# High parts of queries and keys loaded by casting transfers, a third fold in the feature transform, and a new order of the work

## The chip, the cores and the metric

The kernel runs on one core of a Trainium2 chip. The metric is the device time of one execution in microseconds (us); the median of three runs before the change is 947.48 us (945.76 to 948.42). A smaller time is better.

## What is computed

The reference is attention with capped scores, then a two-dimensional Fourier transform added to its input, a normalisation, and a two-layer feed-forward step with a residual. Four batches, 12 heads, 448 tokens, 64 values a head; 768 features, 3072 hidden features.

```python
scores = cap * tanh((q @ k.T) / sqrt(64) / cap)
attn = exp(scores - max(scores)); attn = attn / (sum(attn) + 1e-9)
x = (attn @ v), heads side by side           # 4 x 448 x 768
u = x + real(fft(fft(x, axis=1), axis=2))    # tokens, then features
un = (u - mean(u)) / sqrt(var(u) + 1e-6)     # over the features
out = u + max(un @ w_ch1, 0) @ w_ch2
```

## The kernel before

**Engines.** TensorE (PE in the profile) multiplies, VectorE (DVE) and ScalarE (ACT) do the elementwise work, GpSimd (POOL) does a few small steps, SyncE (SP) issues nearly all transfers. Each engine takes its instructions strictly in the order in which they stand.

**Attention.** The work goes by pairs of heads, 24 of them (`p`). `load_qk` brings queries and keys of a pair (128 x 964 floats) into `qkr`, three buffers deep, `load_v` brings the values. A product in full precision is put together from rounded parts: `split_q` and `split_k` round queries and keys to a high part, `qhl[:, 0]` on VectorE (L312) and `khl[:, 0]` on ScalarE (L310); `rest_q` and `rest_k` subtract it from the full value and so make the low part on VectorE (L315). There are two buffers of `qhl` and of `khl`, used by turns, so the parts of pair p are written into the buffers of pair p - 2, once that pair's scores have been read from them. A pair's 448 keys make seven units of 128 keys for one head or 64 for both; `scores` (L402) computes two units at a time (84 steps `t`), six matmuls each: low keys by high queries, high by low, high by high, summed in PSUM. `tanh` (L412) and `exp` (L415) are one ScalarE instruction each per step. `weigh` (L434) multiplies a unit with the values and a column of ones, `denominators` (L449, L450) and `normalise` (L456) divide.

**Transform, once a batch (six pairs).** The Fourier transforms are matmuls with constant matrices, made smaller by folding the input on its symmetries. `fold_tokens` (L475) and `mirror` (L481) fold tokens and features once; `fold_features` (L489) folds the features a second time, into sums (for even outputs) and differences (for odd outputs). `stage1` (L504) transforms the tokens, `combine` (L310, L524) puts even and odd parts together, `stage2` (L532) transforms the features: for each of its 16 calls, eight matmuls of two passes each, half of them with 192 odd output columns and half with 194 even ones. `add_u` (L552, L556) adds the result; `moments`, `rows`, `standardise` (L565, L574 to L583 on POOL, L610) normalise; `u_cols` (L619) transposes into `xc`, and `operand` and `operand_rest` split that as the queries were split.

**Feed-forward.** 12 groups of hidden features, four batches each: `up` (L745, L756, L757) and `down` (L774, L783). The weights come as raw double words (`raw`, transfer at L651) that the chip turns into a high and a low part: steps `first`, `second` and `third` of each of 96 pieces (L664 to L696, with a cast at L310 on ScalarE).

**Order.** Each step above (`split_q` of a pair, `scores` of two units, one weight step) is a call with a number in the table `ORDER`; the calls are sorted by that number, and so each engine's instructions are put in that order. `at` checks that what a call needs stands ahead of it. The feed-forward work of groups 1 to 11 does not stand in the table; its order follows from a rule that the change leaves alone.

## Time and profile before

| | before |
|---|---|
| median of 3 runs | 947.48 us |
| lowest, highest | 945.76, 948.42 us |
| profiled execution, its time | 947.62 us |
| its span (first to last instruction) | 945.5 us |
| granted TensorE clock, mean | 0.999 |
| TensorE busy | 920.4 us, 97% |
| VectorE busy | 732.4 us, 77% |
| ScalarE busy | 361.5 us, 38% |
| transfers | 64.65 MB |

Busy shares are means over stages that differ: ScalarE's 38% is an engine nearly always busy in the first 210 us and seldom after. A busy time counts an instruction from its start to its end; matmuls overlap, so TensorE can be called busy while the next matmul in line waits a little. How fast a stretch of matmuls goes is better read from many of them without a gap. A releaser (after `<-`) is the instruction or transfer whose end came last before a waiting instruction started.

### The profile page before, as it was taken

The page shows a single profiled execution, that of the slowest core. Times are in us where ns is not written, and L with a number is a line of the kernel's source. Part 1 is how long each engine was busy: PE and PEld are TensorE (multiplying, and loading weights), DVE is VectorE, ACT ScalarE, POOL GpSimd, SP SyncE. Part 2 cuts the span into 40 slices and gives each one's busy share as a digit, 9 for nine tenths or more (in the row PEclk, how much of TensorE's full clock was granted, in tenths as well). Part 3 has the DMA queues.
Part 4 walks back from the last instruction along what each step waited for, and adds up shares of the span by engine and source line. Part 5 has one row for each costly group of instructions (what it writes and reads, how often), then busy time and mean ns, then how long its engine had stood idle before and what let it go on. Part 6 is the DMA issues. An engine that isn't in the chain of part 4 may idle for free.

```text
span 945.5 us, 18375 instructions
## 1 busy us (share of the span) xinstructions
PE 920.4 (97%) x7648; PEld 821.2 (87%) x7648; DVE 732.4 (77%) x1486; ACT 361.5 (38%) x563; POOL 17.0 (2%) x47
## 2 busy tenths in 40 slices
PE   6999999998999999999999999999999999999998
PEld 4777778787888999999999999999999999999997
DVE  3589887899888877787887878778777777768633
ACT  7999999994612212221122211222112221122100
POOL 0000101010100000000000000000000000000000
PEclk9999999999999999999999999999999999999999
DMA  5454332310101211121111211112111211121033
GB/s 152 129 153 135 106 91 54 119 32 20 60 27 51 67 60 51 51 78 51 60 51 51 77 51 51 50 55 64 51 51 51 64 55 51 51 57 60 17 113 122
DMA packets 44914, 64.65 MB, mean 68 GB/s; under 512 B 24608, under 2 KB 29472, under 8 KB 44832
## 3 DMA queue, kind: packets, MB, share of 16 engines
q1 hardware_dynamic: 44752, 63.24, 22.0%
q8 instruction: 60, 0.98, 0.4%
q10 hardware_dynamic: 80, 0.25, 0.1%
q14 instruction: 22, 0.18, 0.1%
HBM read 57.96 MB, written 5.52 MB: 67 GB/s over the span
## 4 chain that ended last, share of the span: by engine, by line
PE 83%; ACT 7%; DVE 7%; issue 2%; DMA 0%; POOL 0%; SPq 0%; DVEq 0%; ACTq 0%; POOLq 0%
PE ph L745 37%; PE po L774 37%; PE av L434 4%; PE s L402 3%; ACT a L412 3%; ACT a L415 2%; PE pq L532 2%; DVE y L524 1%; ACT u L610 1%; DVE bs L565 1%; DVE u L456 1%; DMA capt<-cap 0%; ACT xc L310 0%; ACT khl L310 0%; DVE tf L475 0%
## 5 line engine op out<-in xcount | busy, mean ns | idle before, releaser
L774 PE MATMUL po<-hh,w 128*128 128x448 f32 x1728 | 361.7, 367 | 1.9 <-DVE xc L783 1.4
L745 PE MATMUL ph<-xs,w 128*128 128x448 f32 x1728 | 358.6, 366 | 0.0
L774 PEld LDWEIGHTS po<-hh,w 128*128 128x128 f32 x1728 | 322.9, 188 | 34.2 <-DVE xc L783 5.1
L745 PEld LDWEIGHTS ph<-xs,w 128*128 128x128 f32 x1728 | 323.9, 188 | 27.2 <-issue 0.6
L783 DVE TENSOR_TENSOR xc<-xc,po 128x448 f32<-128x448 f32 x288 | 176.4, 617 | 44.5 <-PE po L774 44.1
L664 ACT ACTIVATE wt<-raw 128x384 f32<-128x384 f32 x96 | 53.4, 557 | 243.5 <-DVE w L696 243.5
L757 DVE SCALAR_TENSOR_TENSOR hh<-ph,hh 128x448 fp32r<-128x448 f32 x96 | 59.9, 624 | 96.2 <-ACT hh L756 95.8
L756 ACT ACTIVATE hh<-ph 128x448 fp32r<-128x448 f32 x96 | 52.3, 545 | 170.0 <-PE ph L745 170.0
L434 PEld LDWEIGHTS av<-vt,a 128*50 128x50 f32 (+3 forms) x3072 | 84.4, 130 | 18.3 <-issue 11.0
L310 ACT CAST w<-wt 128x384 fp32r<-128x384 f32 x96 | 49.2, 513 | 130.2 <-DVE wt L671 130.2
L434 PE MATMUL av<-vt,a 128*50 128x65 f32 (+3 forms) x3072 | 92.0, 223 | 4.0 <-issue 1.7
L402 PE MATMUL s<-qhl,khl 64*128 64x452 f32 (+1 forms) x504 | 78.5, 399 | 11.2 <-DVE khl L315 8.5
L415 ACT ACTIVATE a<-a,capt 128x904 f32<-128x904 f32 x84 | 85.7, 1056 | 0.6
L412 ACT ACTIVATE a<-s,tscale 128x904 f32<-128x904 f32 x84 | 83.4, 1018 | 4.3 <-PE s L402 3.2
L402 PEld LDWEIGHTS s<-qhl,khl 64*128 64x128 f32 (+1 forms) x504 | 50.1, 190 | 26.3 <-DVE khl L315 8.8
L671 DVE SCALAR_TENSOR_TENSOR wt<-wt 128x384 f32<-128x384 f32 x96 | 53.6, 558 | 10.7 <-DVE wt L668 0.9
L668 DVE SCALAR_TENSOR_TENSOR wt<-raw,wt 128x384 uint32<-128x384 uint32 x96 | 53.6, 559 | 3.3
L690 DVE SCALAR_TENSOR_TENSOR wt<-raw,wt 128x384 f32<-128x384 uint32 x96 | 53.6, 558 | 3.3
L696 DVE TENSOR_TENSOR w<-wt 128x384 fp32r<-128x384 f32 x96 | 53.5, 558 | 3.3
L315 DVE TENSOR_TENSOR wt<-wt,w 128x384 f32<-128x384 f32 x96 | 52.8, 550 | 0.7 <-ACT w L310 0.7
L665 DVE TENSOR_SCALAR wt<-raw 128x384 uint32<-128x384 uint32 x96 | 34.1, 355 | 1.2
L687 DVE TENSOR_SCALAR wt<-wt 128x384 uint32<-128x384 uint32 x96 | 33.9, 353 | 0.5
(58 smaller groups left out, 380.6 us busy)
## 6 DMA issues: line engine op xcount, KB each, us to landing
raw<-w2r SPq DMA_DIRECT2D x48, 384.0 KB
raw<-w1r SPq DMA_DIRECT2D x48, 384.0 KB
qkr<-qkT SPq DMA_DIRECT2D x23, 482.0 KB
vt<-vr SPq DMA_DIRECT2D x24, 224.0 KB
outT<-xc SPq DMA_DIRECT2D x24, 224.0 KB
dev<-lnrow SPq DMA_DIRECT2D x4, 224.0 KB
mean<-lnrow SPq DMA_DIRECT2D x4, 224.0 KB
featT<-feat SPq DMA_DIRECT2D x2, 386.0 KB
```

The lines of the kernel that those rows point to most:

```text
L402: nc.tensor.matmul(ps_t[t][:, i, :SQ], khl[p % 2][rows, ik, k0 : k0 + P], qhl[p % 2][rows, iq], start=(k_ == 0), stop=(k_ == 2),)
L412: nc.scalar.activation(a_t[t], ps_t.pop(t)[:, :, :SQ], AF.Tanh, scale=tscale)
L415: nc.scalar.activation(a_t[t], a_t[t], AF.Exp, scale=capt)
L434: nc.tensor.matmul(pa_t[p][q0:q1, j, g * (D + 1) : (g + 1) * (D + 1)], a_t[t][rows, n, OFF[g] + q0 : OFF[g] + q1], vt[rows, p % 2, i], sta ...
L668: nc.vector.scalar_tensor_tensor(tu, hi.bitcast(U32), 0xC0000000, tu, op0=ALU.bitwise_and, op1=ALU.bitwise_or)
L671: nc.vector.scalar_tensor_tensor(t, w, HI_MIN, t, op0=ALU.is_ge, op1=mul)
L690: nc.vector.scalar_tensor_tensor(w, lo, 2.0**-52, w, op0=mul, op1=mul)
L696: nc.vector.tensor_tensor(ws[c][1][:, sl], t, w, op=add)
L745: nc.tensor.matmul(ph[:, :S], w_[:, dc * P : (dc + 1) * P], x_, start=(k_ == 0), stop=(k_ == 3 * NDC - 1),)
L757: nc.vector.scalar_tensor_tensor(hh[:, 1], ph[:, :S], 0.0, f32(hh[:, 0]), op0=ALU.max, op1=sub)
L774: nc.tensor.matmul(po[:, :S], w_[:, dc * P : (dc + 1) * P], hh[:, x_], start=(k_ == 0), stop=(k_ == 3 * GF - 1),)
L783: nc.vector.tensor_tensor(ac, ac, po[:, :S], op=add)
```

## The change

- The high parts of queries and keys are no longer made by ScalarE and VectorE from `qkr`. POOL issues a transfer for each that reads queries or keys from DRAM and casts them on the way into `qhl` and `khl` (48 transfers). The rests still read `qkr`. A cast needs the scores of the pair two before, as before, and no longer the load of `qkr`.
- Within a step of scores the order of the three products is turned: high by high, high keys by low queries, low keys by high queries.
- The even half of the features is folded a third time. `fold_features` does the odd half first; for the even half it folds in place and then makes two sets of 97 columns, by outputs 0, 4, 8, ... and 2, 6, 10, ... `stage1` takes the two sets in its two halves. `stage2` computes 97 even columns from each set, where it summed 194 columns over two halves; they are written to every second column of PSUM, so `add_u` is as before. The constant matrix is filled to match.
- All numbers of `ORDER` are new.

```diff
 ORDER = {
...
     "split_k": [
-        6, 13, 45, 54, 78, 113, 153, 168, 231, 258, 290, 308, 358, 392, 438, 481, 502, 527, 564, 588, 663, 696,
-        742, 761
+        10, 20, 31, 63, 80, 126, 167, 174, 230, 261, 273, 320, 350, 378, 420, 483, 500, 553, 565, 631, 665, 690,
+        751, 768
     ],
...
 ENGINES = {
-    "k": "AAAA",
-    "q": "DDDD",
     "standardise": "AAAA",
...
-            feat[n, :FW, p, NJO : NJO + len(j_even)] = half * f(2 * np.pi * ((d * j_even) % DM) / DM)
             feat[n, :FW, p, :NJO] = half * f(2 * np.pi * ((d * j_odd) % DM) / DM)
+            d, j = np.arange(FW)[:, None], j_even[p::2]
+            feat[n, :FW, p, NJO : NJO + len(j)] = np.where(d == FW - 1, 0.5, 1.0) * f(2 * np.pi * ((d * j) % DM) / DM)
...
     def split_q(p):
-        copy("q", p // NP, qhl[p % 2][:, 0], qk[p][:, :SQ])
+        nc.gpsimd.dma_start(qhl[p % 2][:, 0], qkT[p // NP, PAIRS[p % NP], :, :SQ])
...
     def split_k(p):
-        copy("k", p // NP, khl[p % 2][:, 0], qk[p][:, SQ:])
+        nc.gpsimd.dma_start(khl[p % 2][:, 0], qkT[p // NP, PAIRS[p % NP], :, SQ:])
...
-        terms = (1, 0), (0, 1), (0, 0)
+        terms = (0, 0), (0, 1), (1, 0)
...
-            f_t[b, sd] = new([P, 4, NF], F32, "ff", 2, "ff")
-        t = t_t[b][:R, n]
-        nc.vector.tensor_tensor(
-            f_t[b, sd][:R, 2 * n : 2 * n + 2],
-            t[:, :, :NF],
-            t[:, :, DM // 2 : DM // 4 - 1 : -1],
-            op=(add, sub)[sd != n],
-        )
+            f_t[b, sd] = new([P, 4, 2 * FW], F32, "ff", 2, "ff")
+        t, f, m = t_t[b][:R, n], f_t[b, sd][:R, 2 * n : 2 * n + 2], DM // 4
+        if sd:
+            nc.vector.tensor_tensor(f[:, :, :NF], t[:, :, :NF], t[:, :, 2 * m : m - 1 : -1], op=(add, sub)[n == 0])
+            return
+        nc.vector.tensor_tensor(t[:, :, :m], t[:, :, :m], t[:, :, 2 * m : m : -1], op=(add, sub)[n])
+        for p in range(2):
+            nc.vector.tensor_tensor(
+                f[:, :, p * FW : (p + 1) * FW], t[:, :, :FW], t[:, :, m : FW - 2 : -1], op=(add, sub)[p != n]
+            )
...
-        for sd, (j0, nj) in enumerate(SDJ):
-            for p in range(2):
-                for q0, q1 in ((0, D), (D, R)):
-                    nc.tensor.matmul(
-                        ps[q0:q1, j0 : j0 + nj],
-                        y_t[b, p][:FW, sd, k0 + q0 : k0 + q1],
-                        featT[n][:FW, p, j0 : j0 + nj],
-                        start=(p == 0),
-                        stop=(p == 1),
-                    )
+        for sd, p in (1, 0), (1, 1), (0, 0), (0, 1):
+            out = ps[:, :NJO] if sd else ps[:, NJO + p : NJO + 2 * FW : 2]
+            for q0, q1 in ((0, D), (D, R)):
+                nc.tensor.matmul(
+                    out[q0:q1],
+                    y_t[b, p][:FW, sd, k0 + q0 : k0 + q1],
+                    featT[n][:FW, p, :NJO] if sd else featT[n][:FW, p, NJO : NJO + FW],
+                    start=(sd == 0 or p == 0),
+                    stop=(sd == 0 or p == 1),
+                )
...
-            at(f, p, needs=[("load_qk", p)] + ([(first.__name__, p)] if first else [("scores", u // 2) for u in units(p - 2)]))
+            at(f, p, needs=[("load_qk", p), (first.__name__, p)] if first else [("scores", u // 2) for u in units(p - 2)])
```

What the new order makes of an engine's instructions is shown at three places. A row is source line, operation, output and inputs, shape of the output, and how many follow each other.

ScalarE from its first cast on, before (`khl` are keys, `wt` and `w` a weight piece, `s` scores, `a` the tile of tanh and exp):

```order
L310 CAST khl<-qkr 128x512
L664 ACTIVATE wt<-raw 128x384
L310 CAST khl<-qkr 128x512
L412 ACTIVATE a<-s,tscale 128x904 x2
L415 ACTIVATE a<-a,capt 128x904
L412 ACTIVATE a<-s,tscale 128x904 x2
L415 ACTIVATE a<-a,capt 128x904 x3
```

and with the change (its line numbers are lower by 2 here):

```order
L664 ACTIVATE wt<-raw 128x384
L308 CAST w_113<-wt 128x384
L410 ACTIVATE a<-s,tscale 128x904
L413 ACTIVATE a<-a,capt 128x904
L410 ACTIVATE a<-s,tscale 128x904 x2
L413 ACTIVATE a<-a,capt 128x904
```

The key casts are gone, here and wherever else they stood, and the first weight piece's cast, which stood behind the twelfth tanh, now stands ahead of the first.

VectorE at its first steps for the scores, before (the three `wt` rows are step `first` of a weight piece):

```order
L312 CAST qhl<-qkr 128x452
L315 TENSOR_TENSOR khl<-qkr,khl 128x512
L315 TENSOR_TENSOR qhl<-qkr,qhl 128x452
L665 TENSOR_SCALAR wt<-raw 128x384
L668 SCALAR_TENSOR_TENSOR wt<-raw,wt 128x384
L671 SCALAR_TENSOR_TENSOR wt<-wt 128x384
```

and with the change:

```order
L665 TENSOR_SCALAR wt<-raw 128x384
L668 SCALAR_TENSOR_TENSOR wt<-raw,wt 128x384
L671 SCALAR_TENSOR_TENSOR wt<-wt 128x384
L313 TENSOR_TENSOR qhl<-qkr,qhl 128x452
L313 TENSOR_TENSOR khl<-qkr,khl 128x512
```

The weight steps moved ahead of the two rests.

VectorE in the last batch's transform, from the last token folds (`tf`) on, before (`ff` are the twice folded features, `xs` an operand of the feed-forward step, `y` the transformed tokens):

```order
L475 TENSOR_TENSOR tf<-u 114x4x128 x2
L481 TENSOR_TENSOR tf<-tf 114x2x383
L489 TENSOR_TENSOR ff<-tf 114x386
L481 TENSOR_TENSOR tf<-tf 114x2x383
L489 TENSOR_TENSOR ff<-tf 114x386
L315 TENSOR_TENSOR xs<-xc,xs 128x448
L489 TENSOR_TENSOR ff<-tf 114x386 x2
L524 TENSOR_TENSOR y<-yps,yh 97x2x113 x8
```

and with the change:

```order
L473 TENSOR_TENSOR tf<-u 114x4x128 x2
L479 TENSOR_TENSOR tf<-tf 114x2x383 x2
L488 TENSOR_TENSOR ff<-tf 114x2x193 x2
L490 TENSOR_TENSOR tf<-tf 114x2x192
L492 TENSOR_TENSOR ff<-tf 114x2x97 x2
L490 TENSOR_TENSOR tf<-tf 114x2x192
L492 TENSOR_TENSOR ff<-tf 114x2x97 x2
L313 TENSOR_TENSOR xs<-xc,xs 128x448
L524 TENSOR_TENSOR y<-yps,yh 97x2x113 x4
```

Two of the four folds have become six smaller steps, and the operand's rest moved behind all of them. On TensorE, 18 feed-forward matmuls of group 0 stand ahead of this batch's first feature transform, where 12 stood.

## Rows read from the trace of the kernel before

**Rows 1.** Busy time by stretch: length, busy us (instructions), clock, DMA share, GB/s.
```profile
core 0: us, PE busy (x) PEld busy (x) DVE busy (x) ACT busy (x) POOL busy (x), PEclk, DMA share, GB/s
0.00:9.79 9.79, 1.78 (x8) 1.44 (x10) 3.47 (x12) 3.27 (x6) 0.75 (x7) 1.00 0.76 216
9.79:214.60 204.81, 195.74 (x3985) 159.59 (x3985) 164.87 (x375) 198.05 (x249) 12.40 (x30) 1.00 0.35 102
214.60:300.00 85.40, 80.94 (x519) 70.64 (x515) 75.34 (x151) 30.09 (x57) 3.83 (x10) 1.00 0.11 34
300.00:945.00 645.00, 641.93 (x3148) 589.53 (x3146) 488.68 (x951) 130.10 (x252) 0.00 (x0) 1.00 0.19 60
```

**Rows 2.** Waits of ScalarE, 9.79 to 214.6 us: us in total, times, longest.
```profile
ACT a L412 <- PE s L402: 3.2, 6, 0.8
ACT a L412 <- PE av L434: 0.9, 2, 0.6
```

**Rows 3.** Timeline of ScalarE, two casts and what follows: start us, length us.
```profile
23.74 0.61 ACT L310 CAST khl<-qkr 128x512 fp32r<-128x512 f32 x1
24.25 1.92 ACT L412 ACTIVATE a<-s,tscale 128x904 f32<-128x904 f32 x2
...
31.15 0.54 ACT L310 CAST w<-wt 128x384 fp32r<-128x384 f32 x1
31.55 2.02 ACT L415 ACTIVATE a<-a,capt 128x904 f32<-128x904 f32 x2
```

**Rows 4.** Timeline at the end of attention: last tanh, first feed-forward matmuls.
```profile
211.40 1.00 ACT L412 ACTIVATE a<-s,tscale 128x904 f32<-128x904 f32 x1
...
215.43 1.49 PE L745 MATMUL ph<-xs,w 128*128 128x448 f32 x6
```

**Rows 5.** TensorE without gaps, chain of waits and (third) timeline: start, length, count.
```profile
127.08 3.56 PE av L434 x122
...
133.70 2.76 PE pq L532 x31
...
184.46 1.72 PE L504 MATMUL yps<-seqT,ff 112*64 112x113 f32 x31
...
142.89 1.43 PE s L402 x12
...
251.17 0.79 PE pt L619 x8
```

**Rows 6.** Groups of VectorE's instructions: count, busy us, mean ns, idle before.
```profile
L312 DVE CAST qhl<-qkr 128x452 fp32r<-128x452 f32 x24 | 9.3, 387 | 3.5 <-PE s L402 3.5
L489 DVE TENSOR_TENSOR ff<-tf 114x386 f32<-114x386 f32 x16 | 8.4, 556 | 0.1
L475 DVE TENSOR_TENSOR tf<-u 114x512 f32<-114x512 f32 x24 | 15.9, 683 | 0.2
L315 DVE TENSOR_TENSOR khl<-qkr,khl 128x512 fp32r<-128x512 f32 x24 | 16.4, 682 | 11.4 <-ACT khl L310 11.3
```

**Rows 7.** Timeline of the start, all engines: start us, length us.
```profile
0.72 0.56 ACTq L378 DMA_DIRECT2D qkr<-qkT  x1
...
6.63 0.60 ACT L310 CAST khl<-qkr 128x512 fp32r<-128x512 f32 x1
...
7.87 0.62 DVE L315 TENSOR_TENSOR qhl<-qkr,qhl 128x452 fp32r<-128x452 f32 x1
...
8.41 0.35 DVE L665 TENSOR_SCALAR wt<-raw 128x384 uint32<-128x384 uint32 x1
...
9.47 0.56 DVE L671 SCALAR_TENSOR_TENSOR wt<-wt 128x384 f32<-128x384 f32 x1
9.79 2.15 ACT L412 ACTIVATE a<-s,tscale 128x904 f32<-128x904 f32 x2 [0.34 <-PE s L402]
```

**Rows 8.** Waits of SyncE's queue, whole span: us in total, times, longest.
```profile
SPq L731 <- DMA lnrow<-rowt: 6.4, 3, 3.2
```

**Rows 9.** Timeline of POOL near the end of attention: start us, length us.
```profile
210.21 0.46 POOL L578 TENSOR_TENSOR nt<-nt,var 128x4 f32<-128x4 f32 x1
```

More of the change, by code (lines that the diff above doesn't have):

```diff
@@ L113 @@
     ],
     "fold_tokens": [
-        80, 145, 139, 142, 202, 201, 350, 382, 381, 360, 411, 415, 549, 645, 580, 577, 630, 647, 750, 751, 817,
-        828, 858, 859
+        87, 88, 142, 143, 199, 211, 274, 275, 388, 382, 405, 424, 596, 609, 614, 604, 651, 630, 806, 840, 812,
+        841, 861, 862
     ],
     "load_cap": [
-        2
+        1
     ],
     "load_constant": [
-        287, 150, 196, 189
+        278, 5, 245, 178
     ],
     "load_qk": [
-        1, 8, 21, 15, 66, 101, 124, 157, 169, 229, 181, 307, 346, 355, 427, 440, 441, 492, 488, 514, 662, 666,
@@ L126 @@
-        714, 695
+        3, 18, 34, 51, 91, 118, 132, 172, 205, 194, 192, 296, 363, 305, 326, 437, 490, 556, 459, 608, 682, 621,
+        741, 769
     ],
     "load_v": [
-        11, 24, 81, 92, 122, 129, 186, 214, 232, 265, 311, 378, 398, 406, 503, 542, 556, 578, 596, 687, 734,
-        735, 778, 798
+        8, 42, 81, 85, 136, 152, 175, 207, 222, 258, 353, 380, 383, 429, 468, 537, 577, 592, 603, 689, 740, 756,
+        807, 816
     ],
     "mirror": [
-        207, 203, 413, 417, 654, 653, 860, 865
+        213, 214, 407, 425, 659, 632, 864, 868
@@ L149 @@
-        989, 964, 1013
+        585, 591, 833, 836, 849, 881, 703, 814, 736, 705, 737, 922, 965, 968, 945, 980, 983, 981, 1001, 986,
+        954, 1005, 999, 987
     ],
     "product": [
[3 rows of a table removed]
[3 rows of a table added]
     ],
     "residual": [
-        718, 676, 813, 846, 924, 887, 968, 829, 963, 823, 990, 931, 999, 986, 946, 1009, 1012, 1007, 1005, 1004,
-        1027, 1033, 1036, 1029
+        670, 735, 891, 888, 925, 923, 815, 964, 850, 819, 984, 944, 1007, 969, 948, 1015, 1019, 1021, 1030,
+        1008, 1031, 1006, 1040, 1037
@@ L159 @@
     ],
     "rest_k": [
[L161 to L162 removed]
+        11, 27, 35, 64, 93, 127, 168, 176, 231, 262, 285, 321, 366, 379, 450, 484, 533, 557, 590, 634, 683, 706,
+        755, 770
     ],
     "rest_q": [
[L165 to L166 removed]
+        9, 25, 41, 75, 100, 121, 164, 182, 233, 251, 295, 318, 367, 418, 445, 476, 531, 558, 588, 648, 684, 694,
@@ L167 @@
+        760, 776
     ],
     "row": [
-        573, 809, 944, 1003
+        580, 798, 947, 1004
     ],
     "rows": [
-        349, 553, 835, 920
+        387, 607, 834, 913
     ],
     "rows_cols": [
-        376, 599, 836, 948
+        401, 610, 835, 930
     ],
     "rows_copy": [
-        397, 624, 837, 949
+        402, 620, 837, 931
     ],
     "rows_out": [
-        533, 561, 571, 572, 626, 746, 768, 781, 840, 922, 923, 925, 950, 971, 994, 1002
+        404, 461, 462, 568, 657, 777, 785, 797, 838, 839, 844, 846, 961, 962, 963, 970
@@ L198 @@
-        715, 770
+        6, 24, 40, 66, 99, 108, 135, 181, 228, 237, 293, 299, 356, 403, 444, 464, 498, 523, 587, 647, 653, 675,
+        757, 775
     ],
     "stage1": [
-        219, 271, 234, 274, 458, 459, 447, 434, 724, 726, 685, 701, 880, 882, 878, 885
+        257, 265, 232, 279, 455, 458, 440, 446, 708, 724, 691, 696, 882, 886, 884, 887
     ],
     "stage2": [
-        312, 316, 297, 298, 479, 513, 512, 537, 738, 744, 745, 777, 888, 890, 893, 894
+        322, 329, 290, 291, 511, 507, 534, 536, 732, 733, 767, 758, 893, 894, 903, 908
@@ L236 @@
-        1041, 1042
+        7, 12, 84, 112, 153, 170, 173, 240, 241, 250, 259, 272, 283, 312, 365, 376, 441, 481, 491, 495, 496,
+        504, 512, 673, 698, 919, 920, 921, 937, 941, 982, 988, 989, 1012, 1013, 1014, 1017, 1018, 1029, 1036,
+        1038, 1039
     ],
```

49 lines of the change are left out of this document (20 added, 29 removed), and 46 rows, old and new, of the table ORDER.

## The prediction

> **What bounds the kernel now.** I read the engines' busy time by stage first, then who waits for whom in the stage that the change is made in, and last the single steps of the engine that waits least. By stage the program splits in three, behind a start of 9.79 us [rows 1]. From 300 us on, 3148 feed-forward matmuls take 645 us, 0.205 us each, and TensorE is busy for 641.93 of it: the change has nothing there. From 214.6 to 300 us the last batch's transform runs beside the first feed-forward pieces, TensorE at 80.94 of 85.40 us. From 9.79 us (first tanh) to 214.6 us, attention, the fullest engine is ScalarE: 198.05 of 204.81 us, so 6.8 us idle, most of it for scores or for the product with the values [rows 1, 2]. TensorE's clock is granted in full in all three stretches, so it plays no part.
>
> ScalarE's share there is partly modelled overlap, so I price by step, start to start: the cast of a pair's keys starts at 23.74 us and the next tanh at 24.25 us, 0.51 us; a weight cast starts at 31.15 us and the next exp at 31.55 us, 0.40 us [rows 3].
>
> How near is TensorE? Its own work up to the first feed-forward matmul at 215.43 us [rows 4], by rows in which it ran without a gap: 432 score matmuls on 64 partitions at 1.43/12 us make 51.5, 72 on 128 partitions at 0.205 us make 14.8, 3072 passes with the values at 3.56/122 us make 89.6, 192 passes of the feature transform at 2.76/31 us (0.089) make 17.1, 192 of the token transform at 1.72/31 us (0.055) make 10.7, 48 transposes at 0.79/8 us make 4.7 [rows 1, 5]. Sum 188.4 us, of 207 us from the end of the first rests (8.49 us, below) to 215.43 us. So ScalarE sets the pace and TensorE has some 19 us of waiting, much of it hidden in busy time.
>
> **The change, part by part.**
>
> *Key casts leave ScalarE.* 22 of the 24 lie behind the first tanh: 22 x 0.51 = **-11.2 us** of a path that has nothing else to do. The query casts leave VectorE (0.387 us each [rows 6]); VectorE has 40 us idle in the stretch [rows 1], so that is priced at nothing.
>
> *A weight cast is moved ahead of the first tanh*, as the order of ScalarE shows: one step less later, **-0.4 us**.
>
> *The start.* The three VectorE steps of the first weight piece now stand ahead of both rests. Before, the rests ended at 8.49 us (7.87 + 0.62) and the tanh began at 9.79 us, 1.3 us and six score matmuls later. The three steps span 8.41 to 10.03 us, 1.6 us [rows 7]; without the query cast (0.39) the rests end about 1.2 us later, at 9.7 us. But four of the six matmuls, high by high and high by query rest, are then done, and the last two need a third of 1.3 us: tanh at 10.15 us, **+0.4 us**. Ends: 0, if the weight piece lands early, and +2, if the casting transfers land only when the first load of queries and keys did (6.63 us) and the weight piece later still.
>
> *ScalarE's idle time.* After this ScalarE has some 186 us of steps and TensorE 188.4 - 3.9 = 184.5 us (below), so each now waits for the other more often. If every one of TensorE's 19 us of waiting stayed, its path would shorten by 3.9 us alone, and ScalarE's idle time would grow by 11.2 + 0.4 - 3.9 = 7.7 us; if the waits shrink with ScalarE's work, by nothing. I take a third, **+2.7 us**, since TensorE's waits are largely for ScalarE's own results.
>
> *Third fold.* Of the feature transform 128 passes (64 matmuls, two passes each) shrink from 194 to 97 columns. Between 113 columns (0.055 us) and 193 (0.089 us) a column costs 0.42 ns [rows 5], so a pass saves 0.041 us: 96 passes in attention give 3.9 us, hidden behind ScalarE, and 32 in the last batch give -1.3 us. That the output now goes to every second column, no row prices: between nothing and the whole saving lost; I take nothing, the other transform rows being set by columns. VectorE pays: one piece of 386 elements (0.556 us) becomes one of 384 and two of 194. From 386 to 512 elements it grows by 1.0 ns each [rows 6], so 0.55 + 2 x 0.36 = 1.28 us, +0.72 us, twice a batch. In the first three batches VectorE's 40 us idle hides it; with that cover gone it would be 3 x 1.44 = 4.3 us. In the last it stands between the last weighing and the token transform: +1.44 us, less a rest of 0.6 us that the order moved from within this chain to behind it, +0.8 us. Together **-0.5 us**.
>
> *The casting transfers.* 48 are added, on POOL's queue, 0.49 MB a pair. DMA is at a share of 0.35 with 102 GB/s in attention [rows 1]; 24 x 0.49 MB over 205 us are 58 GB/s more, which at the same ratio brings it to 0.55. POOL's ten small steps a batch stand behind transfers whose waits ended earlier, so they are not held up. Each pair's two transfers wait until the scores of the pair two before have been read. Between that release and the pair's first scores lie three steps of two units (a pair has seven). A step takes (211.40 - 9.79)/83 = 2.43 us now [rows 4, 7], 2.3 us after: 6.9 us, of which the rests need 0.62 + 0.68 [rows 6, 7]. So a pair's casts cost nothing if they land within **5.6 us** of the release. No casting transfer is in the trace. The nearest rows: a small transfer was waited for up to 3.2 us [rows 8]; the first load of queries and keys, as large, was issued at 0.72 us and used at 6.63 us, 5.9 us with two other loads beside it and DMA at a share of 0.76 [rows 1, 7]. I take 4.5 us, between them, since no later stage is as full: **0 us**. The Trainium skill (DMA: Bandwidth & Descriptors, section "Anatomy of one DMA") gives a transfer from GpSimd some 2.0 us plus its bytes at 436 GB/s, by which these would be about 2.5 us each, an estimate; by that the sum is the same, and no run here shows it yet.
>
> Sum: -11.2 - 0.4 + 0.4 + 2.7 - 0.5 = **-9.0 us**. The profiled execution took 947.62 us (span 945.5 us), 0.14 us above the median, so 938.6 us.
>
> **The rivals.**
>
> *Order also closes TensorE's gaps.* TensorE's 19 us of waiting fall to half, and so do the 4.5 us it is idle between 214.6 and 300 us: its first feed-forward matmul comes 3.9 + 9.4 us sooner and the rest shortens by 1.3 + 2.2 us: 930.8 us. For it: everything was placed anew, and six more feed-forward matmuls stand among the last batch's transform. Against it: nothing in the profile says that the waits can be placed away.
>
> *ScalarE's time is handed back.* All of TensorE's waits stay, and score groups stand behind runs of 64 weighings (3.6 us a run): -3.9 from TensorE, -0.5 at the end, and with the start's +2 some 945 us. For it: 184.5 us against 186 us.
>
> *Late casts: slower.* VectorE takes its work in order. If the casts land later than 5.6 us after the release, the rest waits, with the divisions, folds and weight pieces behind it, and TensorE waits in the middle of a score group. Each pair pays what is above 5.6 us, 22 times: at 6.4 us it is 22 x 0.8 = 17.6 us, 956.2 us. It decides from 6.1 us on (22 x 0.54 us takes the 9.0 us and 2.8 more). For it: the one load of this size took 5.9 us. Against it: that was at a DMA share of 0.76, here 0.55; and a step of POOL beside a busy VectorE took 0.46 us, so neither holds the other up for long [rows 9]. The Trainium skill (SBUF — State Buffer, section "SBUF: two separate sides") says that GpSimd cannot write a transfer's descriptors while VectorE runs an operation that uses both its ports, copies and operations with a scalar among them. By that each cast could wait out one such step of the weight pieces, 0.35 us [rows 7], 0.7 us a pair: from 4.5 us to 5.2 us, still inside the window, and where landing is at 5.6 us anyway, 15 us more in all. No run here tests that yet: the step just named ran beside operations of two tensors.
>
> **How the numbers follow.** Forecast 938.6 us (own range 934 to 943): 0.60, as its largest term is plain subtraction from the fullest engine. Gaps closed, 930.8: 0.12. Handed back, about 945: 0.13. Late casts, about 956: 0.15. What a measurement of this kernel can tell from no change is 0.3%, 2.8 us, so "same" is 944.6 to 950.3 us: it holds half of the handed-back case and the mild end of late casts, 0.09. Slower is the rest of late casts, 0.13; faster 0.78. The range reaches down to 929 us for the first rival and up to 947 us, which leaves out most of late casts and little else.
>
> **What would show it.** Right: ScalarE without key casts from the first tanh on, first feed-forward matmul at about 206.5 us, idle ScalarE under 10 us, the passes of 97 columns near 0.05 us, the 645 us after it unchanged. Wrong: rests on VectorE that wait for a transfer, more than 20 us in all, with scores waiting behind them (late casts); ScalarE idle over 14 us, waiting for scores and values (handed back); first tanh after 11 us (start).

## The result and the profile after

The changed kernel is slower: 952.59 us (median of 4 runs, 951.08 to 953.6) beside 947.09 us for the kernel before in the same comparison, a ratio of 1.0057 with a 95% interval of 1.0036 to 1.0078. The forecast was 938.6 us. The profiled execution took 952.05 us, with a span of 950.3 us (945.5 before), so the two traces differ by 4.8 us.

First the windows of the changed kernel's trace that answer to [rows 1] (start, attention, last transform, rest; columns as there):

```profile
0.00:10.66 10.66, 1.54 (x8) 1.41 (x10) 4.38 (x13) 2.76 (x6) 3.12 (x11) 1.00 0.87 220
10.66:216.30 205.64, 196.71 (x3984) 163.12 (x3984) 159.15 (x361) 189.60 (x229) 36.72 (x74) 0.97 0.55 160
216.30:300.00 83.70, 75.66 (x496) 64.96 (x492) 72.41 (x146) 26.85 (x53) 2.85 (x10) 1.00 0.10 30
300.00:950.00 650.00, 646.64 (x3172) 594.24 (x3170) 493.02 (x959) 130.55 (x253) 0.00 (x0) 1.00 0.19 60
```

The last stage is as it was: 650/3172 is 0.205 us a matmul. The DMA share of attention is the 0.55 that was forecast. New is the granted clock of attention, 0.97 where it was 1.00.

Three milestones and the end of the span split the +4.8 us. The first tanh starts at 10.66 us (9.79 before): +0.9. From the first to the last tanh it is 200.10 us (201.61): -1.5. From the last tanh to the first feed-forward matmul, at 217.13 us, it is 6.37 us (4.03): +2.3. From there to the end it is 733.17 us (730.07): +3.1. For the second of these, the window from the first tanh to the end of the last, before and then after:

```profile
9.79:212.40 202.61, 193.54 (x3912) 157.46 (x3910) 162.67 (x371) 195.85 (x247) 12.34 (x30) 1.00 0.35 103
```

```profile
10.66:211.76 201.10, 192.36 (x3880) 158.80 (x3878) 156.62 (x357) 185.09 (x224) 36.72 (x74) 0.97 0.57 163
```

ScalarE's work (the fourth busy time) fell by 10.8 us, as the key casts should make it. Its idle time rose from 6.8 to 16.0 us and took 9.2 of that back. What it waits for, in the same window (columns as in [rows 2], which it answers to):

```profile
ACT a L410 <- PE s L400: 14.4, 13, 3.3
ACT a L410 <- PE av L432: 1.9, 1, 1.9
```

Four of these waits make 9.4 us: 2.70 us at 39.06, 3.34 at 45.29, 1.90 at 93.03 and 1.44 at 97.50. They come in two pairs, and each pair follows one gap on TensorE. The first gap in the timeline of all engines (SPq and POOL issue transfers; khl and qhl are the high parts of the fifth pair):

```profile
26.96 0.55 SPq L379 DMA_DIRECT2D vt<-vr  x1
27.61 0.59 SPq L373 DMA_DIRECT2D qkr<-qkT  x1
28.25 0.43 SPq L651 DMA_DIRECT2D raw<-w2r  x1
28.77 0.86 SPq L373 DMA_DIRECT2D qkr<-qkT  x2
28.85 0.54 POOL L388 DMA_DIRECT2D khl<-qkT  x1 [7.68 <-DVE u L454]
29.38 0.54 POOL L382 DMA_DIRECT2D qhl<-qkT  x1
...
36.38 0.69 DVE L313 TENSOR_TENSOR khl<-qkr,khl 128x512 fp32r<-128x512 f32 x1 [5.52 <-DMA khl<-qkT]
...
37.68 1.34 PE L400 MATMUL s<-qhl,khl 64*128 64x452 f32 x6 [2.37 <-DMA qhl<-qkT]
...
39.06 1.01 ACT L410 ACTIVATE a<-s,tscale 128x904 f32<-128x904 f32 x1 [2.70 <-PE s L400]
...
39.62 3.06 PE L432 MATMUL av<-vt,a 64*64 64x65 f32 x64 [0.61 <-PE s L400]
...
45.29 1.92 ACT L410 ACTIVATE a<-s,tscale 128x904 f32<-128x904 f32 x2 [3.34 <-PE s L400]
```

SyncE's queue stood behind a load of values (vt) until 27 us; then three loads of queries and keys and a weight piece left it together, just as POOL issued the two casts. The one for the keys landed 7.4 us after its issue, the one for the queries 8.2; the medians over all 24 are 4.0 and 3.8 us. VectorE and TensorE waited for them in the middle of their queues. Two more of the 22 pairs behind the start landed late, each with two or three of SyncE's loads starting beside it: the eleventh (issued at 78.66 us) after 6.6 and 6.9 us, the twentieth (160.30 us) after 7.2 and 7.8. The twentieth made TensorE wait for 0.7 us and ScalarE for 0.8; the eleventh comes back below.

What happens to the clock then, in windows of 4 us (columns as above: TensorE's busy time comes second, the granted clock, DMA share and GB/s last):

```profile
30.00:34.00 4.00, 4.00 (x97) 3.21 (x96) 0.86 (x2) 4.00 (x6) 0.00 (x0) 1.00 1.00 337
34.00:38.00 4.00, 1.63 (x40) 1.05 (x32) 1.13 (x2) 2.36 (x4) 1.07 (x2) 1.00 1.05 309
38.00:42.00 4.00, 3.29 (x62) 2.73 (x62) 3.79 (x10) 2.89 (x3) 0.00 (x0) 0.59 0.27 83
42.00:46.00 4.00, 4.00 (x49) 3.14 (x47) 0.03 (x1) 0.71 (x1) 0.00 (x0) 0.56 0.01 2
88.00:92.00 4.00, 2.27 (x28) 1.62 (x24) 3.93 (x11) 2.78 (x4) 0.00 (x0) 1.00 0.36 108
92.00:96.00 4.00, 3.71 (x76) 3.40 (x78) 3.36 (x6) 2.94 (x3) 0.00 (x0) 0.66 0.80 247
208.00:212.00 4.00, 2.37 (x61) 1.60 (x59) 3.15 (x9) 3.97 (x7) 2.58 (x8) 1.00 0.00 0
212.00:216.00 4.00, 4.00 (x96) 3.93 (x98) 2.29 (x5) 4.00 (x5) 0.00 (x0) 0.60 0.02 5
```

Three times in attention TensorE is busy for only 1.6 to 2.4 us of 4, and each time the clock falls to 0.5, the lower of its two levels (1.2 GHz), for a part of the next windows. The second gap has two things at its head, a late cast and a place of VectorE's order. VectorE stands idle for 1.59 us until the eleventh pair's keys land, and then has no wait of its own: the division of pair 8 stands behind that rest, six additions of the transform (L552, then the four of L556 below) and two steps of a weight piece, and the one product buffer (av) is not free before it.

```profile
85.30 0.69 DVE L313 TENSOR_TENSOR khl<-qkr,khl 128x512 fp32r<-128x512 f32 x1 [1.59 <-DMA khl<-qkT]
...
88.39 1.94 DVE L556 TENSOR_TENSOR u<-u,pq 114x384 f32<-114x384 f32 x4
...
90.62 0.31 DVE L687 TENSOR_SCALAR wt<-wt 128x384 uint32<-128x384 uint32 x1
90.96 0.56 DVE L690 SCALAR_TENSOR_TENSOR wt<-raw,wt 128x384 f32<-128x384 uint32 x1
91.44 0.75 DVE L454 TENSOR_TENSOR u<-av,den 114x256 f32<-114x256 f32 x2
...
92.28 1.43 PE L432 MATMUL av<-vt,a 64*64 64x65 f32 x48 [2.02 <-issue]
```

The third, at 210 us, has no cast at its head: the division of pair 22 stands behind an operand's rest and a product with the deviation. The 128 weighings behind it took 5.26 us at the low clock (3.63 us for as many a little earlier), which is most of the +2.3 us.

Last, what TensorE waits for after the first feed-forward matmul:

```profile
PE po L774 <- DVE xc L783: 4.5, 4, 2.0
PE yps L504 <- DVE ff L492: 2.1, 2, 1.6
```

And in the kernel before:

```profile
PE po L774 <- DVE xc L783: 1.4, 3, 0.8
PE yps L504 <- DVE ff L489: 0.7, 1, 0.7
```

### The profile page after: what moved, and what is told of

It reads as the page before. It is cut to its first block, busy times and chain, and to the rows that moved or that the text cites. A ratio compares the mean times of both kernels' runs of the same rounds, so it can differ in the third digit from the quotient of the medians.

```text
span 950.3 us, 18432 instructions
## 1 busy us (share of the span) xinstructions
PE 920.5 (97%) x7648; PEld 823.7 (87%) x7648; DVE 729.0 (77%) x1478; ACT 349.8 (37%) x539; POOL 42.7 (4%) x95
## 4 chain that ended last, share of the span: by engine, by line
PE 88%; DVE 4%; issue 3%; DMA 3%; POOL 2%; ACT 1%; POOLq 0%; DVEq 0%
PE ph L745 36%; PE po L774 36%; PE av L432 6%; PE s L400 5%; DMA qhl<-qkT 2%; PE pq L532 1%; PE yps L504 1%; DMA khl<-qkT 1%; PE pt L619 0%; DVE bs L565 0%; DVE u L556 0%; ACT u L610 0%; POOL ln L576 0%; DVE xc L735 0%; DVE xc L783 0%
## 5 line engine op out<-in xcount | busy, mean ns | idle before, releaser
L432 PEld LDWEIGHTS av<-vt,a 128*64 128x64 f32 (+3 forms) x3072 | 88.9, 135 | 18.1 <-issue 12.8
L432 PE MATMUL av<-vt,a 128*64 128x65 f32 (+3 forms) x3072 | 96.2, 228 | 4.4 <-issue 3.6
L410 ACT ACTIVATE a<-s,tscale 128x904 f32<-128x904 f32 x84 | 83.3, 1012 | 16.4 <-PE s L400 14.4
L671 DVE SCALAR_TENSOR_TENSOR wt<-wt 128x384 f32<-128x384 f32 x96 | 53.6, 559 | 10.8 <-DVE wt L668 0.9
```

What stands on the lines that cost most here:

```text
L410: nc.scalar.activation(a_t[t], ps_t.pop(t)[:, :, :SQ], AF.Tanh, scale=tscale)
L432: nc.tensor.matmul(pa_t[p][q0:q1, j, g * (D + 1) : (g + 1) * (D + 1)], a_t[t][rows, n, OFF[g] + q0 : OFF[g] + q1], vt[rows, p % 2, i], sta ...
L671: nc.vector.scalar_tensor_tensor(t, w, HI_MIN, t, op0=ALU.is_ge, op1=mul)
```

## The experiments

Three theories stood at the start. A: the casts land late when SyncE's loads start with them, and the gaps halve the clock. B: places of the new order make the gaps, whoever makes the high parts. C: the third fold makes the end longer. All times below are medians of 5 to 12 runs; ratios are to the kernel before on the same chip, with their 95% interval (the changed kernel has 1.0057). A percent is 9.5 us.

### One part of the change at a time

**e1_no_casts**: the changed kernel, high parts on the engines again.

```diff
     def split_k(p):
-        nc.gpsimd.dma_start(khl[p % 2][:, 0], qkT[p // NP, PAIRS[p % NP], :, SQ:])
+        copy("k", p // NP, khl[p % 2][:, 0], qk[p][:, SQ:])
...
```

(The same for the queries; both casts have new numbers in `ORDER`, just ahead of their rests.)

> The changed kernel with its order and third fold, but the high parts are made on VectorE (queries) and ScalarE (keys) from the loaded pair again, each cast 0.5 to 6 places ahead of its rest. Theory A (late casts: transfers that land late stop VectorE's and TensorE's queues, and the gaps on TensorE halve its clock): ScalarE gets back 22 x 0.51 = 11.2 us of casts, but its extra idle time of 9.2 us goes; no stretch before 214 us has a granted clock under 0.95; 952.6 + 11.2 - 9.2 = about 954.6 us, range 951 to 957. Theory B (the new order's own places make the gaps, whoever makes the high parts): most of the extra idle time stays, the clock still falls near 92 and 212 us, 952.6 + 11.2 - 3 = about 961 us.

957.5 us, 1.0103 (1.0087 to 1.012). So within the new order the casting transfers are worth some 4.4 us (1.0103 against 1.0057), and the order with the third fold, without them, is 9.8 us slower than before. The clock falls here too, three times (near 38, 158 and 250 us). The first fall stands where the changed kernel has its first gap: SyncE's queue stands behind a load of values until 29 us, the fifth pair's own load of queries and keys leaves at 29.61 us, and ScalarE's cast waits for it with an exp behind it:

```profile
34.56 0.62 ACT L312 CAST khl<-qkr 128x512 fp32r<-128x512 f32 x1 [1.72 <-DMA qkr<-qkT]
```

So the place of SyncE's loads in the new order makes a gap there without any casting transfer too; the late casts make it longer (in the changed kernel the keys' cast, and not the load, is what released VectorE's rest). Neither theory alone: half of each.

**e2_old_fold**: the changed kernel, features folded twice.

```diff
...
-        for sd, p in (1, 0), (1, 1), (0, 0), (0, 1):
+        for sd, (j0, nj) in enumerate(SDJ):
...
```

> The changed kernel with its order and casts, but the features folded twice as before (even outputs from 194 columns over two halves). My prediction priced the third fold at -0.5 us in all: 952.6 + 0.5 = about 953.1 us. Theory C (the third fold's six smaller VectorE steps are what makes the end 3.1 us longer): the time from the first feed-forward matmul to the end falls from 733.2 to about 730.5 us, 949.5 us in all. Theory B (the order makes the end longer): that time stays within 1 us of 733.2.

951.6 us, 1.0037 (1.0023 to 1.0052); its interval meets the changed kernel's. From the first feed-forward matmul to the end it is 732.98 us, as in the changed kernel: in this order the fold is not what makes the end long.

**e3_third_fold**: the kernel before with the third fold alone.

```diff
+ORDER["fold_features"][0:4] = 222, 223, 208, 210
```

(and so on for the other batches: the odd half takes the earlier two numbers; the numbers of `stage1` and `combine` are dealt out anew to match).

> The kernel before with the third fold alone, in the old order (the odd half is folded first, so the four numbers of a batch are dealt out anew). Prediction's price: -0.5 us, 946.6 us, first feed-forward matmul to the end 729.6 us. Theory C: +1.5 to +3 us, 948.6 to 950 us, and the extra time lies behind the first feed-forward matmul.

952.6 us, 1.0053 (1.0037 to 1.007). The fold that the prediction priced at -0.5 us costs 5 us in the old order. Its trace (a run at the low end, 949.75 us) has 733.26 us from the first feed-forward matmul to the end, and there:

```profile
PE yps L510 <- DVE ff L498: 3.7, 2, 3.3
PE po L780 <- DVE xc L789: 1.5, 3, 0.9
```

The token transform waits 3.7 us for the folded features, where it was 0.7 us; behind that the granted clock is 0.60 from 224 to 228 us, and no run tells the two apart. So the end's 3 us have two different sources: the fold's own chain in the old order, and in the new order (e2, the changed kernel) products that wait 4.3 to 4.5 us for VectorE to empty their buffers.

**e4_casts**: the kernel before with casting transfers, each right behind the scores that release it, and with the three products turned.

```diff
-        copy("k", p // NP, khl[p % 2][:, 0], qk[p][:, SQ:])
+        nc.gpsimd.dma_start(khl[p % 2][:, 0], qkT[p // NP, PAIRS[p % NP], :, SQ:])
...
```

> The kernel before with the casting transfers alone (and high by high first), in the old order; each cast is issued as soon as the scores of the pair two before are read. Prediction's price: -11.2 + 2.7 = -8.5 us, about 938.6 us. Theory A (late casts): the casts land 4 to 8 us after their issue here too, VectorE waits for them by 10 us or more in all, the clock falls at least once, and most of the gain is gone: 945 to 955 us. Theory B (the casts are innocent, the new order's places are not): 937 to 941 us, no clock drop, VectorE's wait for casts under 6 us in all.

981.3 us, 1.036 (1.0344 to 1.0376), far beyond what either theory expected. Landing is much as in the changed kernel (keys: 2.8 us at least, median 4.0, 7.8 at most). But the rests stand where a cast of 0.4 to 0.6 us was enough, and twice the casts stand on POOL behind the row statistics of a batch, which themselves wait for VectorE:

```profile
112.06 0.67 POOL L392 DMA_DIRECT2D khl<-qkT  x1 [0.23 <-issue]
...
118.79 1.01 ACT L414 ACTIVATE a<-s,tscale 128x904 f32<-128x904 f32 x1 [6.52 <-PE s L404]
```

That is a wait of 6.5 us for ScalarE at 118.8 us, and one of 6.8 us at 183.6 comes the same way. So the casts can't stand in the old order as it is: there they cost 34 us. How much of the new order they need is not shown by this, and the rest of the 34 us is not divided here.

### The clock

**x0_fill** puts 20 matmuls of the identity matrix, whose result nothing reads, ahead of what I took for the waiting step:

```diff
+        if t == 14:
+            fill = psum.tile([P, 512], F32, tag="d", name="fill")
+            for _ in range(20):
+                nc.tensor.matmul(fill[:, :P], ident, ident, start=True, stop=True)
```

> The changed kernel with 20 matmuls of the identity matrix, about 2.4 us by the rows of 113 columns (0.055 us a pass, two passes each), ahead of the score step that waits for the fifth pair's casts (TensorE idle from about 35.3 to 37.7 us). Nothing reads their result. If the halved clock at 38 to 46 us follows from that gap on TensorE, the granted clock stays at 1.0 there and ScalarE's second wait (3.3 us at 45.3 us) goes, while the first (2.7 us at 39.1 us) stays, as the casts are as late: 952.6 - 3.3 = about 949.3 us. If the clock falls whatever TensorE does in the gap, or ScalarE's second wait comes from the late step alone: 952 to 955 us.

957.6 us, 1.01 (1.0072 to 1.0128): a miss of mine. The order computes step 15 ahead of step 14, so the fill stood behind the gap, ran for 4.86 us in TensorE's way, and the clock fell as before. **z1_fill15** is the same with `if t == 15`.

> The fill of 20 identity matmuls again, now ahead of the score step that does wait for the fifth pair's casts (in x0_fill it stood one step behind it). Nothing reads their result. At the full clock they take 2.4 us (40 passes took 4.86 us at the halved clock in x0_fill), so they fit the 2.4 us gap at 35 to 37.7 us. If the halved clock at 38 to 46 us follows from the gap on TensorE, the clock stays at 1.0 there, ScalarE's second wait (3.3 us at 45.3 us) goes and the first (2.7 us at 39.1 us) stays: 952.6 - 3.3 = about 949.3 us. If it does not follow from the gap: 952 to 955 us and the clock falls all the same.

951.8 us, 1.0045 (1.0026 to 1.0064). In its trace TensorE works through the gap and the clock stays:

```profile
34.00:38.00 4.00, 3.57 (x57) 3.10 (x54) 0.10 (x1) 2.39 (x4) 1.06 (x2) 1.00 1.11 328
38.00:42.00 4.00, 4.00 (x64) 3.49 (x64) 3.64 (x10) 0.56 (x1) 0.00 (x0) 1.00 0.31 94
```

and the 64 weighings that took 3.06 us take 1.76:

```profile
41.32 1.76 PE L436 MATMUL av<-vt,a 64*64 64x65 f32 x64
41.44 1.02 ACT L414 ACTIVATE a<-s,tscale 128x904 f32<-128x904 f32 x1 [5.05 <-PE s L404]
```

With the 12 scores behind them (1.51 instead of 2.63 us) the low clock cost 2.4 of the 6 us of the first gap. That this low clock came of the gap on TensorE is shown; not every gap has one behind it, as the last section says. The time gained little, 1.1 us by the ratios, within both intervals: the fill itself took 4.9 us at the full clock (0.12 us a pass; I had taken x0_fill's for slowed) and held the late scores up, and the two casts landed later still, after 8.9 and 9.3 us. ScalarE has one wait of 5.05 us instead of two of 2.70 and 3.34.

### The transfers

**x2_burst** issues three of SyncE's loads earlier:

```diff
+ORDER["load_qk"][4] = 51.5
+ORDER["fetch"][1] = 51.6
+ORDER["load_qk"][5] = 81.5
```

> The changed kernel with three of SyncE's transfers issued earlier: the loads of pairs 4 and 5 and the second raw weight piece, which in the changed kernel stand behind a load of values until 27 us and then start together with the fifth pair's casts. Theory A (the casts are late because they share the transfer engines with that burst): the casts issued at 28.9 us land within 5 us instead of 7.5 to 8.2, VectorE's 5.5 us wait for keys at 36.4 us shrinks to under 2.5, ScalarE's two waits of 2.7 and 3.3 us go, no halved clock before 90 us: about 952.6 - 6 = 946.6 us. Theory B (the casts are late by themselves): landing stays over 7 us, 952 us.

948.3 us, 0.9998 (0.9981 to 1.0015): 5.6 us by the ratios, near what A gave. The fifth pair's casts land after 5.5 us both, and what is left of the gap, 1.05 us in 4, has no low clock behind it:

```profile
30.00:34.00 4.00, 4.00 (x104) 3.54 (x102) 1.59 (x3) 4.00 (x6) 0.64 (x2) 1.00 0.86 250
34.00:38.00 4.00, 2.95 (x54) 1.91 (x53) 2.72 (x8) 3.89 (x5) 1.06 (x2) 1.00 0.34 70
```

The edit moves the fifth pair's own load too, for which the rests wait as well, so it tells no late cast from a late load. Late casts remain at other places: the pair issued at 51.5 us lands after 6.5 and 7.9 us, the one at 157.7 us after 8.2 and 8.7. The runs lie between 943.2 and 953.0 us, wider than any before; the trace is of the slowest. **z2_sp** gives all of SyncE's loads a regular order, one load of queries and keys behind each load of values:

```diff
+ORDER["load_v"][p] = 0.1 + (number of the last weighing of pair p - 2)
+ORDER["load_qk"][p] = 0.1 + ORDER["load_v"][p - 2]
...
```

(This is the rule; the edit has the numbers, and moves three weight pieces and two constants with them.)

> The changed kernel with SyncE's loads of attention in another order, nothing else: each load of values as soon as its buffer's last weighing stands ahead of it, and behind each exactly one load of queries and keys (two pairs later), with a weight piece or constant at most. Theory A (casts land late when two or three big loads held behind a load of values start with them): every rest's wait for a cast stays under 2.5 us after 30 us, no halved clock before 85 us, ScalarE's waits for scores between 30 and 85 us under 2 us in all: 952.6 - 6 = about 946.6 us, and the runs scatter by under 5 us (x2_burst, with three loads moved, scattered from 943.2 to 953.0). Theory D (casts are late at random, whatever SyncE does): waits of 2 to 3 us at other places, 950 to 953 us.

950.1 us, 1.0021 (1.0004 to 1.0038). No low clock in attention in its trace. The second gap is gone with it, though VectorE's order is untouched: the eleventh pair's keys land after 3.1 us instead of 6.6.

```profile
88.00:92.00 4.00, 3.87 (x85) 3.16 (x83) 3.93 (x11) 3.60 (x6) 0.00 (x0) 1.00 0.90 281
```

Yet only 3.4 us are gained: ScalarE still has a wait of 2.31 us at 50.5 us, one of 2.12 us for a raw weight piece at 72.8, and eight of 0.6 to 1.0 us. **z3_q_vector** makes only the keys by transfer, and the queries' high part on VectorE, right ahead of its rest:

```diff
     def split_q(p):
-        nc.gpsimd.dma_start(qhl[p % 2][:, 0], qkT[p // NP, PAIRS[p % NP], :, :SQ])
+        nc.vector.tensor_copy(qhl[p % 2][:, 0], qk[p][:, :SQ])
```

> The changed kernel with the queries' high parts made on VectorE again (24 x 0.39 us, right ahead of the rest); only the keys' are casting transfers, so 24 of the 48 and 5.6 of 11.9 MB go. Theory A (what is late is a transfer that shares the engines with others): keys land about 1 us sooner, TensorE's wait of 2.4 us for queries at 37.7 us goes, VectorE pays 0.4 us a pair in front of divisions: 948 to 951 us. If the late keys alone set the time: no change, 952 to 953 us. If VectorE's order is as full as its waits suggest: slower, 955 us or more.

953.5 us, 1.0057 (1.0036 to 1.0079): no change that can be told. Half the casting bytes bring the keys' median landing from 4.0 to 3.5 us, but the longest is 7.7, and the first gap stands.

### VectorE's places

**x34_gaps** moves nothing but VectorE's order at the second and third gap (the weight step has a cast on ScalarE that goes with it):

```diff
+ORDER["denominators"][8] = 306.5
+ORDER["normalise"][16:18] = 306.6, 306.7
+ORDER["weights"][13] = 321.5
+ORDER["operand_rest"][4] = 841.3
+ORDER["residual"][8] = 841.5
```

The last two steps have numbers behind the division in the table (849 and 850, against 827). They come behind the last tanh, where the program's second part begins, and in VectorE's instructions they stood ahead of the division all the same; with numbers inside the first part they stay behind it.

> The changed kernel with two places of VectorE's order put right, casts and transfers untouched. At 86 to 92 us the division of pair 8 goes ahead of four additions of the transform and of a weight piece's steps; at 207 to 211 us the division of pair 22 goes ahead of an operand's rest and a product with the deviation. Theory B (these places make TensorE wait for its one product buffer and so halve its clock): ScalarE's waits of 1.9 and 1.4 us near 93 and 97 us go, last tanh to first feed-forward matmul falls from 6.4 to about 4 us, no halved clock at 92 to 96 and 212 to 216 us: 952.6 - 3.3 - 2.3 = 947 us. If the casts set these places too (a rest waits 1.6 us for keys at 85.3 us): 950 to 952 us.

946.7 us, 0.9995 (0.9981 to 1.001): 5.9 us. **w1_gaps_again** is the same edit, for its trace.

> x34_gaps once more (VectorE's two places put right, nothing else), for a trace of it. Theory B: no TensorE gap over 1.5 us and no halved clock near 92 and 210 us; last tanh to first feed-forward matmul about 4 us instead of 6.4; the first gap (casts of the fifth pair, 2.7 and 3.3 us) unchanged: 946 to 948 us. If the 5.9 us of x34_gaps were chance: 950 to 953 us.

944.9 us, 0.997 (0.9953 to 0.9986). Gaps two and three are gone, the clock is full there, and last tanh to first feed-forward matmul is 3.37 us:

```profile
88.00:92.00 4.00, 4.00 (x82) 3.33 (x84) 3.93 (x11) 3.28 (x5) 0.00 (x0) 1.00 0.43 121
92.00:96.00 4.00, 4.00 (x90) 3.51 (x88) 3.96 (x8) 3.94 (x5) 0.00 (x0) 1.00 0.44 113
...
208.00:212.00 4.00, 3.96 (x87) 3.44 (x81) 3.62 (x9) 4.00 (x5) 0.00 (x0) 1.00 0.00 1
```

The first gap is still there (2.34 and 2.62 us of ScalarE's time). The eleventh pair's keys are as late as before (6.5 us, VectorE waits 1.14 us for them), and the second gap closes all the same: the late cast and the place of the division made it together, and in these traces mending either (z2_sp, this one) closed it. So six numbers of the table turn the change from 0.6% slower into 0.3% faster than before; x34_gaps, the same kernel in another comparison, was level with before.

### Repairs together

**x5_all**: x2_burst and x34_gaps, and the first weight piece's VectorE steps behind the rests (`ORDER["weights"][0] = 11.5`, `[1] = 17.5`).

> The changed kernel with the earlier transfers, the two places of VectorE's order, and the first weight piece's VectorE steps behind the first rests. If the four places are all that takes the gain away before the first feed-forward matmul: 952.6 - 6 - 5.6 - 0.9 = about 940 us, ScalarE idle for under 8 us between first and last tanh, no halved clock; the 3 us that the end takes longer than before stay. If the waits only move to other places: 945 to 950 us.

946.4 us, 0.9979 (0.9963 to 0.9996). The gains don't add: 7.4 us, where x2_burst and x34_gaps alone gave 5.6 and 5.9. The casts issued at 51.5 us meet a weight piece and two loads of queries and keys again, the queries land at 60 us, and TensorE's gap of 2.3 us and the low clock come there. The first tanh stays at 10.77 us, as it waits for the first casts' landing (9.1 us), not for the weight steps.

**z4_best**: z2_sp and x34_gaps, the first pair's high parts on the engines, one pair of moments later.

```diff
     def split_k(p):
+        if p == 0:
+            return nc.scalar.copy(khl[0][:, 0], qk[0][:, SQ:])
...
+ORDER["moments"][15] = 916.5
+ORDER["rows"][3] = 916.6
...
```

> All repairs together: SyncE's order of z2_sp, VectorE's two places of x34_gaps, the first pair's high parts made on VectorE and ScalarE (its casts land at 9.0 us, where the kernel before has its first tanh at 9.8), and in the last batch one pair of moments behind two additions of products that TensorE waits for (2.0 us at 243.8 us). By the prices seen so far: -6 for the transfers, -5.6 for the places, -0.9 at the start, -2 to -3.5 at the end: 952.6 - 15 = about 938 us, range 935 to 944. If late casts only move on to other pairs, as in x5_all (58 to 60 us): 944 to 947 us.

947.2 us, 1.0002 (0.9986 to 1.0019). The first tanh is at 9.78 us as in the kernel before, but from the first feed-forward matmul to the end it is still 732.9 us, and a pair issued at 66 us lands after 5.8 and 7.8 us.

**w2_gaps_pair0**: x34_gaps, and the first pair's high parts on the engines as in z4_best.

> VectorE's two places, and the first pair's high parts made on VectorE and ScalarE instead of by casting transfers. First tanh at 9.8 us instead of 10.7 (in z4_best it was 9.78), the rest as w1_gaps_again: 945.8 us, range 944 to 948. If a later start is only made up elsewhere: the same as w1_gaps_again.

947.4 us, 0.9991 (0.9978 to 1.0004). The first tanh is at 11.32 us here, not 9.8: the cap's load landed at 7.8 us, and ScalarE's first cast stands behind it. **w3_end** adds to it later places for steps of the last batch:

```diff
+ORDER["moments"][14:16] = 918.3, 918.5
+ORDER["rows"][3] = 918.6
+ORDER["rows_cols"][3] = 934.5
...
+ORDER["standardise"][12:16] = 934.1, 934.3, 934.2, 934.4
```

> w2_gaps_pair0 with the last batch's last two moments, its row statistics and the four normalising steps behind the four additions that empty the product buffers. If the order's places in the last batch are the cause (TensorE's 4.5 us of waiting for these additions in the changed kernel, 1.4 before): that wait falls to under 2 us, first feed-forward matmul to end 730.5 to 731.5 us instead of 733.2, 2 us less than w2_gaps_pair0. If the third fold's longer chain on VectorE is the cause: no change, 733 us.

949.4 us, 1.0015 (1.0004 to 1.0027), 2 us slower than w2_gaps_pair0. The wait it aimed at shrinks, and another takes its place:

```profile
PE rt L608 <- POOL ln L601: 3.3, 1, 3.3
PE po L794 <- DVE xc L803: 2.5, 3, 0.9
```

The statistics of the last batch are now what TensorE waits for. So the end's 3 us can't be had by moving these steps alone.

**w4_burst_end**: w3_end with x2_burst's three loads earlier and the next loads in their pairs' order.

```diff
+ORDER["load_qk"][7:11] = 132.2, 152.2, 175.2, 207.2
+ORDER["load_constant"][3] = 152.4
```

> w3_end with seven loads of queries and keys and one weight piece and one constant issued earlier, so that no more than one big load starts within 2 us of a pair's casts before 60 us. If late casts still take time: the 6 us of ScalarE's waits at 39 and 45 us go and nothing takes their place, 938 to 941 us. If a late cast's 6 us are handed back by TensorE's other waits (z2_sp kept 2 to 5 us of the 6): 942 to 945 us.

946.7 us, 0.9986 (0.9973 to 0.9999). ScalarE's waits for scores between the first and the last tanh:

```profile
ACT a L435 <- PE s L425: 12.8, 15, 1.6
```

No wait is longer than 1.6 us and there is no gap at 35 us, but the sum is hardly less than the changed kernel's 14.4 us. The late casts are not gone either: the pair issued at 156 us lands after 7.3 and 8.1 us, TensorE waits 1.46 us for its queries at 165.06 us, and the clock is 0.73 from 164 to 168 us.

## Why the prediction was wrong

**What bounds the kernel.** "TensorE's clock is granted in full in all three stretches, so it plays no part" is the first step that failed. It was true of the trace of before [rows 1] and I took it for a property of the stretches. In the changed kernel attention ran at 0.97, with the low level behind three gaps.

**Key casts, -11.2.** Right: with the weight cast (-0.4) ScalarE's steps shrank by 10.8 us. With the next term the forecast had attention, first to last tanh, 8.9 us shorter; it measured 1.5.

**ScalarE's idle time, +2.7, between 0 and 7.7.** This term is the step that cost most of the forecast: it measured +9.2. (A third of 7.7 is 2.6, not 2.7.) My upper end let TensorE keep the waits that it had; 9.4 us come from two gaps that were not there before, each paid for twice, once as a wait and once as a slow stretch behind it. One gap is late transfers behind SyncE's held-up queue, the other a late transfer and a place of VectorE's order together.

**Casting transfers, 0.** The landing was right in the middle (4.5 us taken, 4.0 and 3.8 measured), and the window of 5.6 us nearly: for the fifth pair it was 5.1, from the issue at 28.85 us to TensorE's last work at 35.31, less two rests. What failed is the step from a typical landing to a price: pairs are not alike. Of the 22 behind the start 19 land inside 5.6 us and three need 6.6 to 8.2, where SyncE's loads start with them; of these the first costs 6 us (a part of which the late load alone would cost, e1_no_casts), the second 1.6 us of VectorE's time ahead of the second gap, the third 0.8 us. The rival "late casts" had the sign, and nearly the size (956), but it priced every pair a little instead of one pair heavily; its sign, rests that wait for more than 20 us in all, was not quite met (17.0 us for casts behind the first tanh). The estimate of 2.5 us a transfer from the Trainium skill (DMA: Bandwidth & Descriptors, "Anatomy of one DMA") was near the shortest landings, 2.8 and 2.9 us; with other transfers beside them the trace has landings up to 8.2 us. The other section of the Trainium skill that the prediction cites (SBUF — State Buffer, "SBUF: two separate sides") would have POOL's descriptors wait for VectorE's copies; the 24 issues for the keys took 0.53 to 0.65 us each, so nothing of it is seen in POOL's own time; whether a part of a late landing is such a wait, no run here tests.

**ScalarE's time handed back.** I gave it 0.13 and some 945 us. Its sign was met: ScalarE was idle for 16.0 us, over 14. And 945 us is about what the mended kernels reach: 944.9 to 947.4 us for every combination that mends the second and third gap but w3_end, with 12 to 14 us of idle ScalarE in w1_gaps_again (196.65 us with 184.78 busy) and w4_burst_end (199.32 with 185.69), against 6.8 us before. My forecast of 938.6 us was not reached by the median of any. But that this is time handed back is argued and not shown: the traces of w1_gaps_again, w2_gaps_pair0, w4_burst_end, x5_all and z4_best each still have a cast that lands only after 7.8 to 8.8 us.

**From the last tanh on.** I had no term for the way from the last tanh to the first feed-forward matmul; the third gap cost 2.3 us there. The last batch was priced at -0.5 us and measured +3.1: the matmuls of 97 columns did get cheaper (32 passes, half of them of 97 columns, in 2.18 us, where 31 took 2.76 [rows 5]), and the fold's chain cost about what I said in the new order (the wait for folded features grew by 1.4 us, by 0.5 with the old fold in e2_old_fold), but products that wait for additions behind the moments' steps cost 3.1 us more, and the view of the new order that I rested on stopped ahead of them.

**The start, +0.4.** +0.9, inside its ends; the reason was another, the first casts landing at 9.0 us and not the weight steps ahead of the rests (x5_all).

**What stays open.** I can't divide the changed kernel's 5.5 us exactly between the transfers and the places: a repair of either alone gives 3.4 to 8.2 us, both together 5.2 to 7.4. Which waits in w4_burst_end and z4_best belong to the remaining late casts and which to TensorE having nearly as much work as ScalarE, no run separates; none has every cast inside the window. Why the places of the last batch cost 3 us in the new order is read from the trace alone, as w3_end only put another wait in their place. Nor does the trace name a cause for some waits of TensorE in the middle of a run of weighings (2.03 us at 49 us in z2_sp, 1.72 us at 54.8 us in the kernel before). A third buffer for the high parts, which would widen the window, was not tried.

## What to carry to other kernels

A transfer that takes the place of an engine's step is priced by its slowest landing at each place where it is waited for, and by what else starts with it: look for a queue that is held behind one wait and then lets several loads go. Where TensorE runs without gaps, price a new gap with the low clock that may follow it: of the 6 us that the first gap cost here, 2.4 were the low clock. Where two engines have nearly the same work, a step taken off the one is worth far less than its length; ask first how much the other has left.

## What the hardware showed that I had not expected

- In the changed kernel the granted clock fell to 0.5 behind three gaps, TensorE being busy for 1.6 to 2.4 us of 4, and stayed there while TensorE was busy again (0.50 in 40 to 44 us at 4.00 us busy of 4). Filling the gap with useless matmuls kept it at 1.00 (z1_fill15). Not every such gap does it: a wait of 2.04 us at 243.8 us in the changed kernel had no low clock behind it, while x5_all's wait of as much at 238.2 us did; and x2_burst's trace, with TensorE busy for 2.37 us from 88 to 92 us, stays at 1.00 behind it.
- Casting transfers of 0.23 and 0.26 MB landed between 2.8 and 8.2 us after their issue in one execution, the latest three pairs behind the start where two to four of SyncE's loads started beside them. The kernels that depend on this scatter more from run to run: x2_burst by 9.7 us, the kernel before by 5 us.
